# Two attentions on one core: how the projections load x and weights

## The chip, the cores and the metric

The kernel runs on one NeuronCore of a Trainium2 chip. The core has five engines with instruction streams of their own: TensorE (PE: matmuls; its weight loads are listed apart as PEld), VectorE (DVE), ScalarE (ACT), GpSimd (POOL) and SyncE (SP, which here only issues DMAs). Engines wait for one another through semaphores, and each runs its own stream strictly in order. The metric is the device time of one execution in microseconds (us); less is better.

## What is computed

Two attention layers over 2048 rows of width 576, each with 32 heads of 18, on different inputs; the outputs stand side by side. A is a multi-query attention: one key head and one value head serve all 32 query heads. B is cut into 4 segments of 512 rows: within a segment causal attention, and beside it a memory M that earlier segments' keys and values have filled.

```python
q = heads(x @ wq); k = x @ wk; v = x @ wv                        # A
o = softmax(q k^T * Dh**-0.5) v
a = o @ wo

q, k, v = heads(x @ wq), heads(x @ wk), heads(x @ wv)            # B
for s in range(4):
    a_dot = softmax(qs ks^T * Dh**-0.5 + causal) vs
    a_mem = (phi(qs) M) / (phi(qs) z + 1e-6)
    o = g * a_mem + (1 - g) * a_dot                              # g = sigmoid(beta)
    M, z = M + phi(ks)^T vs, z + sum(phi(ks))
b = o @ wo
```

## The kernel before

It has two phases. The *projections* make q, k and v of A and B and write most of them to DRAM; this ends near 320 us. The *attention* phase follows, with an order of instructions written out by hand. The change touches the first only, in which a scheduler orders the instructions of each engine: it may move a DMA or an operation to another place in its engine's stream, ahead of or behind work of neighbouring steps.

**Precision.** Each fp32 operand is split in two parts (fp32r): the cast (high part) and the difference (low part). x gives `xh` and `xl`, weights give `wAh`, `wAl` (A) and `wBh`, `wBl` (B). The contraction over 576 runs in blocks k = 0 to 4 of 128 rows, the last of them 64 rows, loaded twice so that high and low part share it. `proj` (L201, its matmuls at L208) therefore makes an output tile of up to 126 x 512 by 14 matmuls: three for each of k = 0 to 3 (high by high, low x by high weight, high x by low weight) and two for k = 4.

**Loading x.** `next_x(xT, c)` (L186) allocates `xh` and `xl` for 512 rows and returns a function that loads one block k: `load_xk` (L175) takes one of three `xr` buffers of 128 x 512, starts the DMA on SP (L179), casts on DVE (L180) and subtracts on DVE (L182; L184 for k = 4, where there are two DMAs of 64 rows).

**Loading weights.** `load_wk` (L192) takes one of two `wr` buffers, starts the DMA on SP (L195), casts on ACT (L196) and subtracts on POOL, or on DVE for A's first weights (L197).

**A, chunks c = 0 to 3 of 512 rows** (from L221). For c = 0 the five blocks of weights and x are loaded and split in turn. Then five tiles t = 4, 0, 1, 2, 3, each: 14 matmuls into a PSUM tile `pj` (4 buffers); for t = 4 the magnitude (L237), a copy of the values (`vT`, L239) and four transposes (L242); the absolute value for a bound on ACT (`AQ`, L244); `split2` (L106: cast on ACT at L110, subtraction on DVE at L111) into `qp` (2 buffers), and `store_parts` (L114), a DMA on SP at L115. After each tile one block of the next chunk's x is loaded and split, and in chunks 2 and 3 also one block of B's weights (columns 504 to 1152 and 1152 to 1728). At the end of chunk 0 ACT issues the constants (L257 to L262), a row of ones to DRAM (L263, from `onest`) and five tiny loads of beta (L267), and takes beta's exponential (L270).

**Boundary from A to B.** A small matmul with `sel` (L280), DVE operations for `kbdA` (L284), 20 matmuls (L289), and from their result the shift, split in parts (L120 to L123) and stored by four DMAs on ACT (L295).

**B, segments s = 0 to 3** (from L325). Five tiles of keys and queries: 14 matmuls each, the column magnitude `kmB` (L360) and its product with a mask (L364), `split2`, stores, and `phi` (L308 and L309 on ACT, L311 on DVE) whose result `kf` is transposed by PE (L338) and copied (L339). In segment 0 one more block of weights (columns 0 to 504) is loaded after each tile. Then the values (L396 to L401), transposes of the last key head (L409), and four query tiles.

At the very start PE runs nine matmuls on a tile of zeros (`zero`, L160).

Of the kernel before, what the change touches and what calls it, by code (L numbers as in the profile page):

```python
# [7 lines left out]
F32 = mybir.dt.float32  # L8
# [4 lines left out]
ALU = mybir.AluOpType  # L13
# [7 lines left out]
C = 512  # L21
# [47 lines left out]
def attention_pair_kernel(ctx, tc, a_xT, a_w, a_wo, b_xT, b_w, b_wo, b_beta, ident_d, hmask_d, bmask_d, cmask_d, sel_d, zmask_d, selx_d, sely_d, out):  # L69
# [75 lines left out]
    with ExitStack() as ph:  # L145
# [2 lines left out]
        pt = ph.enter_context(tc.tile_pool(name="pt", bufs=2))  # L148
        ps = ph.enter_context(tc.tile_pool(name="ps", bufs=1, space=PSUM))

        onest = pt.tile([32, 128], F32, name="onest", bufs=1)
        nc.gpsimd.memset(onest, 1.0)


        zero = pt.tile([128, C], F32, name="r1", bufs=2)
        nc.vector.memset(zero, 0.0)
        zero = zero.bitcast(BF)
        pz = ps.tile([128, C], F32, name="nd", bufs=2)
# [10 lines left out]
        def halves(k):  # L169

            if k < 4:
                return [(slice(0, 128), slice(128 * k, 128 * k + 128))]
            return [(slice(0, 64), slice(512, 576)), (slice(64, 128), slice(512, 576))]

        def load_xk(xh, xl, xT, c, k):  # L175
            t0 = c * C
            xr = px.tile([128, C], F32, name="xr", bufs=3)
            for rows, src in halves(k):
                nc.sync.dma_start(xr[rows], xT[src, t0 : t0 + C])  # L179
            nc.vector.tensor_copy(xh[:, k], xr)  # L180
            if k < 4:
                nc.vector.tensor_tensor(xl[:, k], xr, xh[:, k].bitcast(F32), op=ALU.subtract)  # L182
            else:
                nc.vector.tensor_tensor(xh[64:128, k], xr[64:128], xh[64:128, k].bitcast(F32), op=ALU.subtract)  # L184

        def next_x(xT, c):  # L186

            xh = px.tile([128, 5, C], F32R, name="xh")
            xl = px.tile([128, 4, C], F32R, name="xl")
            return xh, xl, lambda k: load_xk(xh, xl, xT, c, k)  # L190

        def load_wk(wh, wl, w, c0, n, k, first):  # L192
            wr = pt.tile([128, 648], F32, name="wr", bufs=2)
            for rows, src in halves(k):
                nc.sync.dma_start(wr[rows, :n], w[src, c0 : c0 + n])  # L195
            nc.scalar.copy(wh[:, k, c0 : c0 + n], wr[:, :n])  # L196
            (nc.vector if first else nc.gpsimd).tensor_tensor(  # L197
                wl[:, k, c0 : c0 + n], wr[:, :n], wh[:, k, c0 : c0 + n].bitcast(F32), op=ALU.subtract
            )
# [20 lines left out]
        kAp = p1.tile([128, 1], F32, name="kAp")  # L220
        for c in range(NCH):  # L221
            if c == 0:
                xh, xl, fillx = next_x(a_xT, 0)
                for k in range(5):
                    load_wk(wAh, wAl, a_w, 0, CA, k, True)
                    fillx(k)
                nc.sync.dma_start(ident, ident_d)
            else:
                xh, xl = nx[:2]
            nx = next_x(a_xT, c + 1) if c < NCH - 1 else next_x(b_xT, 0)  # L230
            for t in (4, 0, 1, 2, 3):
                M = 114 if t == 4 else 126
                pj = ps.tile([128, C], F32, name="pj", bufs=4)
                proj(pj[:M], wAh, wAl, xh, xl, 126 * t, M)
                R = RT[t]
                if t == 4:
                    nc.vector.tensor_reduce(km[:M, c : c + 1], pj[:M], axis=AX.X, op=ALU.max, apply_absolute_value=True)  # L237
                    vT = p1.tile([128, C], F32, name="vT", bufs=2)
                    nc.scalar.copy(vT[96:114], pj[96:114])  # L239
                    pv = ps.tile([128, 4, 128], F32, name="tr", bufs=1)  # L240
                    for i in range(4):
                        nc.tensor.transpose(pv[:, i, 0:DH], vT[96:114, 128 * i : 128 * i + 128], ident[96:114, 96:114])  # L242
                    nc.vector.tensor_copy(VAv[:, 4 * c : 4 * c + 4, 1:VW], pv[:, :, 0:DH])
                nc.scalar.activation(AQ[:R, t, c * C : c * C + C], pj[:R], AF.Abs)  # L244
                R2 = 90 if t == 4 else 126
                qp = split2(pt, pj[:R2], R2)
                store_parts(qp, 0, R, qA[c], H0[t], HT[t])
                nx[2](t)

                if c == 2:  # L250
                    load_wk(wBh, wBl, b_w, 504, 648, t, False)
                if c == 3:
                    load_wk(wBh, wBl, b_w, 2 * D, D, t, False)
                if t == 4:
                    nc.sync.dma_start(kA[:, :, c * C : c * C + C], qp[72:90].bitcast(F32))
            if c == 0:
# [3 lines left out]
                nc.scalar.dma_start(zmask[:126], zmask_d)  # L260
                nc.scalar.dma_start(selx[:126], selx_d)
                nc.scalar.dma_start(sely, sely_d)  # L262
                nc.scalar.dma_start(ones_d.rearrange("j (a b) -> (j a) b", b=128), onest)  # L263
                nc.vector.memset(gt, 0.0)
                for t in range(5):
                    lo, nh = H0[t], HT[t]
# [33 lines left out]
        Mbd = p2.tile([128, 5, 7, VW], F32, name="Mbd")  # L300
        Mst = p2.tile([128, 5, 7, DH], F32, name="Mst")
        zst = p2.tile([128, 5, 32], F32, name="zst")
        zc = p2.tile([128, 5], F32, name="zc")

        def phi(src, R, nm, bufs):
# [19 lines left out]
        for s in range(NSEG):  # L325
            xh, xl = nx[:2]
            last = s == NSEG - 1
            if not last:
                nx = next_x(b_xT, s + 1)
            kmB = p2.tile([128, 5], F32, name="kmB", bufs=2)  # L330
            kbB = p2.tile([128, 5, 32], BF, name="kbB", bufs=2)
            pkN = p2.tile([128, 5, 4, 126], F32, name="pkN")
# [24 lines left out]
            for t in range(5):  # L357
# [9 lines left out]
                    store_parts(qp, 72, 54, kB[s], 28, 3)  # L367
                    magnitude(4, pj)
                if s == 0:
                    load_wk(wBh, wBl, b_w, 0, 504, t, False)  # L370
                elif not last:
                    nx[2](t)
                if not last or t == 4:
# [660 lines left out]
```

## Time and profile before

| what | value |
| --- | --- |
| runs | 1475.27, 1481.17 and 1477.9 us, median 1477.9 |
| profiled execution, its own time | 1475.97 us |
| its span in the profile | 1474.3 us |
| projections | 0 to about 320 us |
| attention phase | from there to the end |

The profile is one execution. A window's row gives, for a stretch of time, each engine's busy time with its number of instructions, the granted TensorE clock (1.00 is full), the mean busy share of the 16 DMA engines and the GB/s that they moved. A wait's row names the waiting engine and line, what released it, and the waits' total, number and longest, in us. A timeline row is start, duration, engine (a q behind its name is its queue of DMA issues), line, operation, output and input; in brackets the idle time ahead of it and what ended it. A group's row has the number of instructions, their busy time in us and mean in ns, and the idle time before them with what ended it. In the page's slices each digit is the busy tenth of one fortieth of the span.

### The profile page before, as it was taken

The page shows a single profiled execution, that of the slowest core. Times are in us where ns is not written, and L with a number is a line of the kernel's source. Part 1 is how long each engine was busy: PE and PEld are TensorE (multiplying, and loading weights), DVE is VectorE, ACT ScalarE, POOL GpSimd, SP SyncE. Part 2 cuts the span into 40 slices and gives each one's busy share as a digit, 9 for nine tenths or more (in the row PEclk, how much of TensorE's full clock was granted, in tenths as well). Part 3 has the DMA queues.
Part 4 walks back from the last instruction along what each step waited for, and adds up shares of the span by engine and source line. Part 5 has one row for each costly group of instructions (what it writes and reads, how often), then busy time and mean ns, then how long its engine had stood idle before and what let it go on. Part 6 is the DMA issues. An engine that isn't in the chain of part 4 may idle for free.

```text
span 1474.3 us, 40745 instructions
## 1 busy us (share of the span) xinstructions
PE 1428.2 (97%) x17540; PEld 838.0 (57%) x17540; DVE 1031.0 (70%) x1209; ACT 1193.5 (81%) x1424; POOL 256.0 (17%) x311
## 2 busy tenths in 40 slices
PE   7989999998999999999999999999999999999988
PEld 5768878764544555555555555555555555555554
DVE  6574664555767668887777787777778877887841
ACT  3334334248999999999999999999999999999950
POOL 1031000001134413511110270131115200100010
PEclk9999999999999999999999999999999999999999
DMA  6775643446346345432322343123203121110111
GB/s 197 250 241 179 188 152 122 155 156 192 119 137 200 90 124 160 152 108 86 96 79 75 95 139 105 54 92 98 78 28 120 56 65 49 42 53 17 33 66 62
DMA packets 87985, 166.31 MB, mean 113 GB/s; under 512 B 12479, under 2 KB 21241, under 8 KB 87625
## 3 DMA queue, kind: packets, MB, share of 16 engines
q1 hardware_dynamic: 81510, 157.82, 34.5%
q10 hardware_dynamic: 6291, 5.85, 1.2%
q8 instruction: 138, 2.26, 0.7%
q14 instruction: 46, 0.38, 0.1%
HBM read 96.15 MB, written 67.49 MB: 111 GB/s over the span
## 4 chain that ended last, share of the span: by engine, by line
PE 61%; ACT 9%; DMA 4%; issue 2%; DVE 1%; SPq 1%; POOL 0%; DVEq 0%; POOLq 0%; ACTq 0%
PE O L810 28%; PE E L762 18%; PE F L660 12%; ACT P L780 9%; PE E L771 3%; DMA stB<-qB 2%; PE E L660 1%; DMA oB<-oe 1%; DMA stB<-kB 1%; SPq L586 0%; DVE osb L684 0%; DMA stA<-qA 0%; DVE W L777 0%; PE O L660 0%; DVE oe L819 0%
## 5 line engine op out<-in xcount | busy, mean ns | idle before, releaser
L780 ACT ACTIVATE P<-E 128x1024 f32<-128x1024 f32 (+1 forms) x800 | 784.3, 1068 | 19.7 <-PE E L762 11.2
L777 DVE COPY W<-E 128x1024 f32<-128x1024 f32 (+1 forms) x384 | 461.0, 1200 | 192.4 <-PE E L762 123.4
L810 PE MATMUL O<-P,VA 128*32 128x256 f32 x7936 | 509.2, 380 | 4.9 <-DVE oe L819 4.9
L780 ACT ACTIVATE P<-W 128x1024 f32<-128x1024 f32 (+1 forms) x384 | 430.7, 1122 | 3.3 <-DVE W L777 3.1
L810 PEld LDWEIGHTS O<-P,VA 128*32 128x32 f32 x7936 | 261.9, 110 | 152.8 <-issue 10.8
L762 PE MATMUL E<-stA,kstA 56*128 56x512 f32 x1920 | 328.7, 439 | 1.9 <-ACT P L780 1.0
L762 PEld LDWEIGHTS E<-stA,kstA 56*128 56x128 f32 x1920 | 154.6, 184 | 177.2 <-ACT P L780 113.6
L785 POOL TENSOR_SCALAR_AFFINE_SELECT P<-P 128x256 f32<-128x256 f32 (+1 forms) x192 | 93.7, 493 | 423.0 <-ACT P L780 390.3
L660 PE MATMUL F<-woB,o 126*32 126x192 f32 (+1 forms) x1920 | 127.4, 338 | 0.3 <-DVE osb L684 0.3
L742 DVE SCALAR_TENSOR_TENSOR q<-q,PD 128x1024 f32<-128x1024 f32 x96 | 118.3, 1232 | 0.0
L660 PE MATMUL F<-woA,o 126*32 126x192 f32 (+2 forms) x1480 | 88.7, 337 | 5.8 <-DVE osb L684 5.8
L810 PE MATMUL O<-P,vseg 128*32 128x256 f32 (+2 forms) x1536 | 83.7, 348 | 1.9 <-POOL P L785 1.8
L644 POOL TENSOR_TENSOR o<-oc,rb 126x512 f32<-126x512 f32 (+1 forms) x20 | 26.2, 1323 | 341.6 <-PE F L660 248.3
L110 ACT CAST qp<-pj 126x512 fp32r<-126x512 f32 (+1 forms) x56 | 32.6, 584 | 63.0 <-DVE kmB L360 45.2
L660 PEld LDWEIGHTS F<-woB,o 126*32 126x32 f32 (+1 forms) x1920 | 38.2, 108 | 71.8 <-issue 62.1
L819 DVE COPY oe<-O 128x512 f32<-128x512 f32 x64 | 44.3, 692 | 49.2 <-PE O L810 42.5
L111 DVE TENSOR_TENSOR qp<-pj,qp 126x512 fp32r<-126x512 f32 (+1 forms) x56 | 38.2, 687 | 54.4 <-ACT qp L110 54.2
L208 PE MATMUL pj<-xh,wBh 128*126 128x512 f32 x180 | 73.8, 414 | 2.1 <-DVE xh L180 2.1
L208 PE MATMUL pj<-xh,wBl 128*126 128x512 f32 x180 | 72.9, 405 | 0.0
L771 PE MATMUL E<-stB 56*128 56x256 f32 (+3 forms) x512 | 62.9, 352 | 6.9 <-DMA stB<-kB 2.8
L810 PEld LDWEIGHTS O<-P,vseg 128*32 128x32 f32 x1536 | 48.6, 110 | 28.7 <-POOL P L785 3.9
L660 PEld LDWEIGHTS F<-woA,o 126*32 126x32 f32 (+1 forms) x1480 | 34.8, 108 | 51.9 <-issue 34.6
(135 smaller groups left out, 1439.9 us busy)
## 6 DMA issues: line engine op xcount, KB each, us to landing
stB<-kB SPq DMA_DIRECT2D x96, 144.0 KB
stB<-qB SPq DMA_DIRECT2D x32, 288.0 KB
stA<-qA SPq DMA_DIRECT2D x30, 288.0 KB
oA<-oe SPq DMA_DIRECT2D x32, 256.0 KB
oB<-oe SPq DMA_DIRECT2D x32, 256.0 KB
qA<-qp SPq DMA_DIRECT2D x16, 504.0 KB
kB<-qp SPq DMA_DIRECT2D x16, 504.0 KB
qB<-qp SPq DMA_DIRECT2D x16, 504.0 KB
```

What stands on the lines that cost most here:

```text
L110: nc.scalar.copy(qp[:R, 0, :n], src)
L111: nc.vector.tensor_tensor(qp[:R, 1, :n], src, qp[:R, 0, :n].bitcast(F32), op=ALU.subtract)
L208: nc.tensor.matmul(dst, w[:, c0 : c0 + M], x, start=i == 0, stop=i == len(ops) - 1)
L660: nc.tensor.matmul(dst[32 * j : 32 * j + 32], parts[ab, c][: RT[t], t, r0 : r0 + 32], wo[ab][: RT[t], t, c0 : c0 + n], start=start, stop=stop,
L742: steps.append(lambda a=a: v.scalar_tensor_tensor(q, q, a, p, op0=ALU.add, op1=ALU.mult))
L762: nc.tensor.matmul(e[:, j], kstA[rows, 128 * kt : 128 * kt + 128], st[rows, h, :], start=True, stop=True)
L771: nc.tensor.matmul(e[:, j, c0 : c0 + 512 - 128 * k], st[rows, 4 + h, ks], st[rows, h, 128 * k :], start=True, stop=True)
L777: nc.vector.tensor_copy(src[:, :, :n], e[:, :, :n])
L780: nc.scalar.activation(p[:, :, :n], src[:, :, :n], AF.Exp, scale=SCALE)
L785: nc.gpsimd.affine_select(diag, diag, pattern=[[0, 2], [0, m], [1, 128]], base=0, channel_multiplier=-1, compare_op=ALU.is_ge, fill=0.0)
L810: nc.tensor.matmul(o[32 * j : 32 * j + 32, q0 : q0 + n], v, p[:, j % 2, p0 : p0 + n], start=m == hf == 0, stop=last and hf == 1,)
L819: nc.vector.tensor_copy(osb, o)
```

## The change

- x: a new `raw_x` allocates one `xr` tile for all five blocks of 512 rows (128 x 5 x 512, one buffer) and starts its six DMAs on SP together, at the beginning of the chunk or segment before the one that uses it (for chunk 0: in turn with its weights). `next_x` only casts and subtracts, at the places where load and split stood.
- Weights: `raw_wk` starts the loads on ACT's queue, all five blocks of a group together, into five buffers (`wr` in pool `p1` for A's weights and the first two groups of B's, `qf` in `p2` for the third). They stand at the beginning of chunks 2 and 3 and of segment 0; `split_wk` does the cast and the subtraction at the old places.
- Room: `vT` has one buffer instead of two; the tile of zeros takes the name `sht` with one buffer; `onest` is made and stored at the start of B instead of at the start of the kernel and the end of chunk 0.

The arithmetic is the same.

```diff
         pt = ph.enter_context(tc.tile_pool(name="pt", bufs=2))
         ps = ph.enter_context(tc.tile_pool(name="ps", bufs=1, space=PSUM))
-        onest = pt.tile([32, 128], F32, name="onest", bufs=1)
-        nc.gpsimd.memset(onest, 1.0)
-        zero = pt.tile([128, C], F32, name="r1", bufs=2)
+        zero = pt.tile([128, C], F32, name="sht", bufs=1)
         nc.vector.memset(zero, 0.0)
         zero = zero.bitcast(BF)
         pz = ps.tile([128, C], F32, name="nd", bufs=2)
...
                 return [(slice(0, 128), slice(128 * k, 128 * k + 128))]
             return [(slice(0, 64), slice(512, 576)), (slice(64, 128), slice(512, 576))]
-        def load_xk(xh, xl, xT, c, k):
-            t0 = c * C
-            xr = px.tile([128, C], F32, name="xr", bufs=3)
-            for rows, src in halves(k):
-                nc.sync.dma_start(xr[rows], xT[src, t0 : t0 + C])
-            nc.vector.tensor_copy(xh[:, k], xr)
-            if k < 4:
-                nc.vector.tensor_tensor(xl[:, k], xr, xh[:, k].bitcast(F32), op=ALU.subtract)
-            else:
-                nc.vector.tensor_tensor(xh[64:128, k], xr[64:128], xh[64:128, k].bitcast(F32), op=ALU.subtract)
-        def next_x(xT, c):
+        def raw_x(xT, c, engine, parts=range(5)):
+            xr = px.tile([128, 5, C], F32, name="xr", bufs=1)
+            def load(k):
+                for rows, src in halves(k):
+                    engine.dma_start(xr[rows, k], xT[src, c * C : c * C + C])
+            for k in parts:
+                load(k)
+            return xr, load
+        def next_x(xr):
             xh = px.tile([128, 5, C], F32R, name="xh")
             xl = px.tile([128, 4, C], F32R, name="xl")
-            return xh, xl, lambda k: load_xk(xh, xl, xT, c, k)
-        def load_wk(wh, wl, w, c0, n, k, first):
-            wr = pt.tile([128, 648], F32, name="wr", bufs=2)
+            def fill(k):
+                nc.vector.tensor_copy(xh[:, k], xr[:, k])
+                if k < 4:
+                    nc.vector.tensor_tensor(xl[:, k], xr[:, k], xh[:, k].bitcast(F32), op=ALU.subtract)
+                else:
+                    nc.vector.tensor_tensor(xh[64:128, k], xr[64:128, k], xh[64:128, k].bitcast(F32), op=ALU.subtract)
+            return xh, xl, fill
+        def raw_wk(wr, w, c0, n, k):
             for rows, src in halves(k):
-                nc.sync.dma_start(wr[rows, :n], w[src, c0 : c0 + n])
+                nc.scalar.dma_start(wr[rows, :n], w[src, c0 : c0 + n])
+            return wr
+        def split_wk(wr, wh, wl, c0, n, k, first):
             nc.scalar.copy(wh[:, k, c0 : c0 + n], wr[:, :n])
             (nc.vector if first else nc.gpsimd).tensor_tensor(
                 wl[:, k, c0 : c0 + n], wr[:, :n], wh[:, k, c0 : c0 + n].bitcast(F32), op=ALU.subtract
...
         kAp = p1.tile([128, 1], F32, name="kAp")
         for c in range(NCH):
             if c == 0:
-                xh, xl, fillx = next_x(a_xT, 0)
+                xr, loadx = raw_x(a_xT, 0, nc.sync, ())
+                xh, xl, fillx = next_x(xr)
                 for k in range(5):
-                    load_wk(wAh, wAl, a_w, 0, CA, k, True)
+                    loadx(k)
+                    wr = raw_wk(p1.tile([128, 648], F32, name="wr", bufs=5), a_w, 0, CA, k)
+                    split_wk(wr, wAh, wAl, 0, CA, k, True)
                     fillx(k)
                 nc.sync.dma_start(ident, ident_d)
             else:
                 xh, xl = nx[:2]
-            nx = next_x(a_xT, c + 1) if c < NCH - 1 else next_x(b_xT, 0)
+            nx = next_x((raw_x(a_xT, c + 1, nc.sync) if c < NCH - 1 else raw_x(b_xT, 0, nc.sync))[0])
+            if c > 1:
+                w0, wn = ((504, 648), (2 * D, D))[c - 2]
+                wrs = [raw_wk(p1.tile([128, 648], F32, name="wr", bufs=5), b_w, w0, wn, k) for k in range(5)]
             for t in (4, 0, 1, 2, 3):
                 M = 114 if t == 4 else 126
                 pj = ps.tile([128, C], F32, name="pj", bufs=4)
...
                 R = RT[t]
                 if t == 4:
                     nc.vector.tensor_reduce(km[:M, c : c + 1], pj[:M], axis=AX.X, op=ALU.max, apply_absolute_value=True)
-                    vT = p1.tile([128, C], F32, name="vT", bufs=2)
+                    vT = p1.tile([128, C], F32, name="vT", bufs=1)
                     nc.scalar.copy(vT[96:114], pj[96:114])
                     pv = ps.tile([128, 4, 128], F32, name="tr", bufs=1)
                     for i in range(4):
...
                 nx[2](t)
                 if c == 2:
-                    load_wk(wBh, wBl, b_w, 504, 648, t, False)
+                    split_wk(wrs[t], wBh, wBl, 504, 648, t, False)
                 if c == 3:
-                    load_wk(wBh, wBl, b_w, 2 * D, D, t, False)
+                    split_wk(wrs[t], wBh, wBl, 2 * D, D, t, False)
                 if t == 4:
                     nc.sync.dma_start(kA[:, :, c * C : c * C + C], qp[72:90].bitcast(F32))
             if c == 0:
...
                 nc.scalar.dma_start(zmask[:126], zmask_d)
                 nc.scalar.dma_start(selx[:126], selx_d)
                 nc.scalar.dma_start(sely, sely_d)
-                nc.scalar.dma_start(ones_d.rearrange("j (a b) -> (j a) b", b=128), onest)
                 nc.vector.memset(gt, 0.0)
                 for t in range(5):
                     lo, nh = H0[t], HT[t]
...
         Mbd = p2.tile([128, 5, 7, VW], F32, name="Mbd")
         Mst = p2.tile([128, 5, 7, DH], F32, name="Mst")
         zst = p2.tile([128, 5, 32], F32, name="zst")
+        onest = p2.tile([32, 128], F32, name="onest")
+        nc.gpsimd.memset(onest, 1.0)
+        nc.scalar.dma_start(ones_d.rearrange("j (a b) -> (j a) b", b=128), onest)
         zc = p2.tile([128, 5], F32, name="zc")
         def phi(src, R, nm, bufs):
...
             xh, xl = nx[:2]
             last = s == NSEG - 1
             if not last:
-                nx = next_x(b_xT, s + 1)
+                nx = next_x(raw_x(b_xT, s + 1, nc.sync)[0])
+            if s == 0:
+                wrs = [raw_wk(p2.tile([128, C], F32, name="qf", bufs=5), b_w, 0, 504, k) for k in range(5)]
             kmB = p2.tile([128, 5], F32, name="kmB", bufs=2)
             kbB = p2.tile([128, 5, 32], BF, name="kbB", bufs=2)
             pkN = p2.tile([128, 5, 4, 126], F32, name="pkN")
...
                     store_parts(qp, 72, 54, kB[s], 28, 3)
                     magnitude(4, pj)
                 if s == 0:
-                    load_wk(wBh, wBl, b_w, 0, 504, t, False)
+                    split_wk(wrs[t], wBh, wBl, 0, 504, t, False)
                 elif not last:
                     nx[2](t)
                 if not last or t == 4:
```

## The prediction

> **What bounds the kernel now.** I read the page's first two parts, then the seven stages up to 320 us by windows, then each engine's waits in the first 125 us, then the order of instructions of both kernels.
>
> ```profile
> span 1474.3 us, 40745 instructions
> PE 1428.2 (97%) x17540; PEld 838.0 (57%) x17540; DVE 1031.0 (70%) x1209; ACT 1193.5 (81%) x1424; POOL 256.0 (17%) x311
> PE   7989999998999999999999999999999999999988
> ```
> ```profile
> 0.00:30.35 30.35, 22.97 (x83) 15.10 (x84) 18.71 (x35) 10.03 (x16) 3.92 (x8) 0.94 0.71 201
> 30.35:47.23 16.88, 16.87 (x75) 13.15 (x74) 10.20 (x18) 6.85 (x12) 0.32 (x1) 1.00 0.67 211
> 47.23:64.64 17.41, 17.12 (x76) 12.98 (x75) 8.90 (x16) 6.87 (x12) 0.00 (x0) 1.00 0.75 236
> 64.64:84.48 19.84, 17.25 (x75) 13.06 (x74) 13.99 (x17) 8.11 (x14) 7.87 (x5) 1.00 0.74 234
> 84.48:106.52 22.04, 17.28 (x79) 11.67 (x78) 16.96 (x33) 8.32 (x15) 7.32 (x6) 0.92 0.81 268
> 106.52:123.00 16.48, 15.71 (x95) 14.21 (x96) 12.47 (x20) 8.68 (x22) 4.15 (x4) 0.90 0.72 222
> 123.00:320.00 197.00, 197.00 (x1071) 155.15 (x1069) 104.58 (x234) 69.73 (x143) 1.05 (x3) 1.00 0.48 154
> ```
>
> TensorE (PE) bounds the whole: 97% busy. The first four rows are the A chunks 0 to 3, the fifth is the boundary from A to B up to the first transposes of B's phi keys (L338), the sixth the rest of B's segment 0 up to L409. The columns after the length are PE, weight loads, VectorE (DVE), ScalarE (ACT), GpSimd (POOL), then granted clock, DMA share and GB/s. Length less PE's busy time: 7.4, 0.0, 0.3, 2.6, 4.8, 0.8, 0.0 us; 15.8 us idle before 123 us and none from there to 320. At half clock PE counts as busy, so what the clock cost is apart: 0.06, 0.08 and 0.10 of stages one, five and six, some 1.7 us in each.
>
> In the order of the two kernels all five engines run the same sequence from the L409 transposes on. So what the change brings must be decided before 123 us; after that it is a shift. Its ceiling is 15.8 + 3 x 1.7, about 21 us (1.4%).
>
> ```profile
> PE tr L338 <- DVE kf L311: 3.1, 2, 2.6
> PE pj L208 <- DVE xh L180: 2.9, 4, 1.9
> PE pj L208 <- ACT wAh L196: 2.3, 2, 1.2
> PE pj L208 <- DVE xl L182: 1.5, 1, 1.5
> PE pj L208 <- DVE qp L111: 1.4, 1, 1.4
> ```
>
> These are PE's waits (us in total, times, longest). Late x blocks (L180, L182) cost 4.4, late weights 2.3; the phi chain at the boundary (L311) 3.1, and that is no load at all.
>
> **The change, part by part.**
>
> *Chunk 0.* All five w blocks get buffers of their own and go out on ACT's queue; SP carries x alone.
>
> ```profile
> 1.26 0.42 SPq L179 DMA_DIRECT2D xr<-a_xT  x1
> 6.30 0.49 PE L208 MATMUL pj<-xh,wAh 128*114 128x512 f32 x1 [1.09 <-ACT wAh L196]
> 9.45 1.29 DVE L182 TENSOR_TENSOR xl<-xr,xh 128x512 fp32r<-128x512 f32 x2
> 11.36 0.43 DVE L180 CAST xh<-xr 128x512 fp32r<-128x512 f32 x1 [0.62 <-DMA xr<-a_xT]
> 13.04 1.52 DVE L197 TENSOR_TENSOR wAl<-wr,wAh 128x618 fp32r<-128x618 f32 x2 [0.53 <-ACT wAh L196]
> 13.87 1.22 SPq L195 DMA_DIRECT2D wr<-a_w  x2
> 18.09 0.71 ACT L196 CAST wAh<-wr 128x618 fp32r<-128x618 f32 x1 [0.82 <-DMA wr<-a_w]
> 20.00 0.69 DVE L184 TENSOR_TENSOR xh<-xr,xh 64x512 fp32r<-64x512 f32 x1
> ```
> ```profile
> 64.00:76.00 12.00, 10.49 (x45) 7.71 (x43) 6.92 (x8) 2.73 (x6) 3.38 (x2) 1.00 0.87 288
> 76.00:80.00 4.00, 2.92 (x15) 2.29 (x15) 3.21 (x4) 3.95 (x8) 1.59 (x1) 1.00 0.19 41
> 40.02 0.39 PE L208 MATMUL pj<-xh,wAl 128*126 128x512 f32 x1
> 40.25 0.39 PE L208 MATMUL pj<-xh,wAh 128*126 128x512 f32 x1
> ```
>
> Today the fifth weight block is issued only at 13.87 (two buffers) and cast at 18.09. Changed: x of 5 x 256 KB and three w of 309 KB (from the tiles' shapes) leave at once, 2.2 MB; at the 288 GB/s of a crowded stretch that is 7.7 us, landed near 9.2. The other two w leave behind ACT's first casts, near 9.4; by today's 13.87 to 18.09 they can be cast 4.2 us on, 13.6, before DVE comes to them. DVE's new order puts the fill of x block 3 ahead of the first wAl, so PE, after its first few matmuls at 6.3, stands until 9.2 + 0.43 + 0.76, about 10.4. The fourth wAl is the ninth DVE operation from 9.2 on: casts of 0.43 twice, wAl of 0.76 four times (1.52 for two), xl of 0.65 twice (1.29 for two), 0.69 once: 5.9, so 15.1. After it come 49 of the chunk's 74 matmuls, one per 0.23 us (40.02 to 40.25): 11.3, end 26.4. The new gap of 3.7 us is longer than any of PE's waits above, and I expect a half-clock spell behind it like the three of today: 1.7, end 28.1. Against 30.35: -2.2. Bounds: no spell and landing 1 us earlier -5.0; a spell and landing 2 us later 0.
>
> *Chunk 1.*
>
> ```profile
> ACT gt L270 <- DMA gt<-b_beta: 3.4, 1, 3.4
> ACT wBh L196 <- DMA wr<-b_w: 17.3, 6, 5.5
> ACT qp L110 <- DMA qA<-qp: 11.2, 8, 2.8
> SPq L195 <- POOL wBl L197: 6.4, 6, 2.4
> ```
>
> The beta loads are now issued behind the weights, the last one among chunk 0's evacuations in ACT's order, so they land near the chunk's end; the exponential on ACT (L270, a 3.4 us wait today in the idle start) waits for them in front of evacuations. Four pj buffers give three tiles' lead, 3 x 14 x 0.23 = 9.7 us, so a wait of that size is covered; +0.2 for tiles that meet a thin lead, bounds 0 (the chunk has no idle to give) and +3.4 (the wait bare).
>
> *Chunks 2 and 3.* Today the B weights are issued one tile ahead, after POOL's split freed a buffer (6.4 us of waits on SP), and ACT stands 17.3 us for them. Changed, the five blocks go out far ahead, from ACT. x for the next 512 rows goes out as one group at the chunk's start; its single buffer is free once the last fill of the chunk before is done. The hole from 76 to 80 us (DMA share 0.19) between crowded stretches shows that today's transfers are late by order of issue, not by bytes. Floor for both chunks: twice chunk 1's 16.87 is 33.7 against 37.25, -3.5. I take -2.8: one thin wait per chunk stays. Bounds 0 and -3.5. Moved issues: 18 of b_w at 0.42 are 7.6 us from SP's queue to ACT's, over stages in which ACT is busy 6.9 to 8.3 of 17 to 22 us; covered.
>
> *Boundary.*
>
> ```profile
> 84.48 0.28 PE L280 MATMUL mm<-kmx,sel 114*126 114x1 f32 x2
> 85.54 1.26 PE L289 MATMUL nd<-AQ,kbdA 126*32 126x512 bf16 x20
> 96.01 0.96 PE L208 MATMUL pj<-xh,wBh 128*126 128x512 f32 x3 [1.92 <-DVE xh L180]
> 103.16 0.68 DVE L111 TENSOR_TENSOR qp<-pj,qp 126x512 fp32r<-126x512 f32 x1
> 106.52 0.62 PE L338 MATMUL tr<-ident,kf 126*128 126x126 f32 x4 [2.62 <-DVE kf L311]
> L360 DVE TENSOR_REDUCE kmB<-pj 126x1 f32<-126x512 f32 x5 | 3.4, 687 | 0.5 <-PE pj L208 0.5
> L239 ACT COPY vT<-pj 18x512 f32<-18x512 f32 x4 | 2.3, 578 | 2.9 <-DVE km L237 2.9
> ```
>
> With x present, PE runs from T (84.48 today) through L280 and L289 (1.5) and four key tiles (56 x 0.23 = 12.9): done at T+14.4 without the 1.92 us wait and the spell behind it. But DVE's new order puts the kmB reduction of the fourth tile (0.69) and its small product (0.2) ahead of the first tile's qp subtraction; from that subtraction to the transposes passes 106.52 - 103.16 = 3.4 today. T+18.7, against T+22.04; I add 0.3 for semaphores: -3.0. The stall at L338 itself thus grows, 2.6 to about 4.5 us: DVE's order is late next. On ACT six w issues, the moved ones_d store and four shA stores stand ahead of the first B evacuation; at 0.42 each 4.6 us, done well before T+14. Bounds: +2.0 (two of those stores wait as the 3.2 us below), -6.5 (the 4.8 idle and 1.7 of clock all gone, which DVE's order nearly forbids).
>
> *The rest to 123 us*: one half-clock spell today, one after: 0, bounds +1.5 and -1.7. Memset, vT's single buffer and the renamed zero tile: 0, one operation each in engines with idle time; vT, if bare, 0.6.
>
> **Sum:** -2.2 + 0.2 - 2.8 - 3.0 + 0 = -7.8. The profiled execution took 1475.97 us (its span 1474.3 and 1.7 around it), 1.9 below the median 1477.9 of runs from 1475.27 to 1481.17. 1477.9 - 7.8 = **1470**.
>
> **The rivals.**
>
> *R1: the DMA engines set the pace.* GB/s times length give 14.7 MB for chunks 2, 3 and the boundary; at 288 GB/s that is 51 us, against 53.5 by my sum (33.7 + 0.7 + 19.0 + rounding) and 59.3 today. For it: hardly any slack, and a share of 0.81 already. Against: part of it can go earlier, into chunk 1 with its 0.67. If transfers keep today's mean pace (14.7 MB in 59.3 us, 248 GB/s), these stages gain nothing and chunk 0 alone is left: -2.2 + 0.2, 1476. The Trainium skill, DMA: Bandwidth & Descriptors, "Issuing engines are not separate DMA queues", says that DMAs started by scalar, sync or gpsimd share the same 16 DMA engines, so another queue saves only sequencer time; no run yet shows which holds here, and by it R1 would be the outcome.
>
> *R2: it doesn't load ahead.* One x buffer instead of three blocks: the next group can't leave before the last fill, 1.3 MB take 4.6 us at 288 GB/s, and the first fill comes one tile (3.2 us) into a chunk. DVE then stands some 2 us per chunk; the pj lead of 9.7 hides one such stand, which is against it. Where they come through bare, four groups (chunks 1 to 3 and B's first) give back 4 x 2 = 8 and the time is 1478.
>
> *R3, slower: ACT stands behind its DMA issues.*
>
> ```profile
> 96.64 0.68 ACT L196 CAST wBh<-wr 128x576 fp32r<-128x576 f32 x1 [4.30 <-DMA wr<-b_w]
> 100.50 0.59 ACT L110 CAST qp<-pj 126x512 fp32r<-126x512 f32 x1 [3.18 <-DMA shA<-shp]
> ```
>
> Each issue waits for an earlier transfer to release its completion semaphore and, on ACT, holds the evacuations behind it, hence the pj buffers, hence PE. Waits of 3 to 4 us on transfers occur on ACT today. A stage leaves ACT about 10 us; six issues fit while each waits under 1.6 us. At 3.2 each, three stages lose 3 x (19.2 - 10) = 27.6, less the 9.7 of lead once: +17.9, less chunk 0's 2.2 and the boundary's 3.0: 1477.9 + 12.7, about 1490. Against it: in the new order most of these semaphores belong to transfers issued a whole tile before.
>
> *R4, more:* no spell in chunk 0 and none behind the boundary stall: -7.8 - 3.4 and chunks 2, 3 at the floor -0.7: 1466.
>
> **How the numbers follow.** Within 0.5% (7.4 us: 1470.5 to 1485.3) is about what a measurement can't tell from no change. Forecast 0.52 (own range 1466 to 1474; just over half of it under 1470.5), R4 0.13, R1 0.14, R2 0.08, R3 0.13. Faster: 0.30 + 0.13 = 0.43; same: 0.22 + 0.14 + 0.08 = 0.44; slower 0.13. Range: all lower bounds together are -16.7, 1461; R4's own spread ends near 1463, and above, 1484 leaves R3 out: 1462 to 1484.
>
> **What would show it.** Right: chunk ends near 28, 45, 62, 80 us; a PE gap from about 6.7 to 10; x fills gone from PE's waits after chunk 0; the L338 wait on L311 at 4 to 5 us; L338 near 99 and L409's stage unchanged. R1: DMA share over 0.9 in chunks 2 and 3 with waits on x or weights. R3: ACT's largest waits on DMA in front of L244 or L110, and PE waiting for qp's chain. Wrong altogether: any change in PE's busy share after 123 us.

## The result and the profile after

The changed kernel took 1484.5 us (median of 6 runs, 1482.3 to 1485.5) against 1476.8 us for the kernel before (6 runs, 1474.5 to 1481.2): ratio 1.0043 with a 95% interval of 1.0027 to 1.006, slower by 0.4%. The forecast was 1470, in a range of 1462 to 1484. The profiled execution of the changed kernel has a span of 1482.1 us, 7.8 more than the one before.

Windows of the changed kernel, cut where PE begins chunks 1, 2, 3, the boundary (the matmul with `sel`, now L294), the first phi transposes (now L357) and the transposes of the last key head (L409 before, now L428). Columns as in the windows before. Some lines have new numbers in the changed kernel: a weight's load, cast and subtraction are L201, L205 and L206, x's load and cast L178 and L190, the matmuls of `proj` L217, the copy `vT` and its transposes L254 and L257, `AQ` L259, phi's last step L328.

```profile
0.00:29.18 29.18, 25.21 (x83) 16.95 (x84) 16.77 (x33) 8.65 (x13) 0.29 (x5) 1.00 0.63 180
29.18:49.95 20.77, 17.24 (x76) 12.80 (x74) 12.35 (x20) 9.83 (x18) 6.26 (x4) 1.00 0.88 278
49.95:72.99 23.04, 19.09 (x74) 14.90 (x75) 13.16 (x17) 8.79 (x16) 10.27 (x7) 0.85 0.79 254
72.99:89.76 16.77, 16.77 (x75) 13.15 (x74) 9.71 (x19) 6.83 (x12) 0.00 (x0) 1.00 0.61 197
89.76:110.59 20.83, 14.73 (x80) 10.86 (x78) 14.68 (x33) 5.92 (x12) 2.99 (x4) 0.96 0.88 272
110.59:129.36 18.77, 16.11 (x91) 14.36 (x92) 8.08 (x13) 8.67 (x20) 3.75 (x3) 0.86 0.68 215
129.36:325.00 195.64, 195.41 (x1057) 153.25 (x1054) 102.91 (x230) 69.84 (x144) 1.05 (x3) 1.00 0.44 143
```

Stage by stage against the kernel before:

| stage | before, us | after, us | difference | predicted |
| --- | --- | --- | --- | --- |
| chunk 0 | 30.35 | 29.18 | -1.2 | -2.2 |
| chunk 1 | 16.88 | 20.77 | +3.9 | +0.2 |
| chunks 2, 3 | 17.41, 19.84 | 23.04, 16.77 | +5.6, -3.1 | -2.8 together |
| boundary, to the first phi transposes | 22.04 | 20.83 | -1.2 | -3.0 |
| to the last key head's transposes | 16.23 | 18.77 | +2.5 | 0 |
| the rest of the span | 1351.55 | 1352.74 | +1.2 | 0 |

Chunk 3 runs without a gap; chunks 1 and 2 pay for it, and more. Of chunk 2's 5.6 us, 3.7 are idle time of PE and 2.0 are pace: PE was busy for 19.09 us with 74 matmuls in place of 17.12 with 76, and the granted clock was 0.85 in place of 1.00, behind a gap of 3.9 us. Times of the last key head's transposes and of a small matmul at the end of the projections, the first two rows before, the others after:

```profile
122.75 0.50 PE L409 MATMUL tr<-ident,kn 128*18 128x128 f32 x3 [0.28 <-DVE pkN L339]
317.74 0.27 PE L319 MATMUL nd<-ident,fm 128*1 128x128 f32 x1
```
```profile
129.36 0.49 PE L428 MATMUL tr<-ident,kn 128*18 128x128 f32 x3
325.02 0.27 PE L336 MATMUL nd<-ident,fm 128*1 128x128 f32 x1
```

6.6 us at the first point, 7.3 at the second, 7.8 at the end: most of it is decided before 130 us.

PE's waits in the first 130 us of the changed kernel:

```profile
PE tr L357 <- POOL wBl L206: 6.1, 1, 6.1
PE tr L257 <- ACT vT L254: 3.9, 1, 3.9
PE pj L217 <- DVE qp L111: 3.5, 2, 2.4
PE tr L357 <- DVE kf L328: 2.6, 1, 2.6
PE pj L217 <- DVE wAl L206: 1.9, 1, 1.9
```

The waits for x have left PE's list. They have not left the kernel: DVE, which casts the next chunk's x among other work, stands 16.2 us for it in the first 130 us, and stood 13.7 before. What came in their place are waits for evacuations (qp, vT, phi). Two chains of the timeline show how the first two stalls in A come about:

```profile
26.14 0.68 ACTq L281 DMA_DIRECT2D gt<-b_beta  x1
33.07 0.21 ACT L284 ACTIVATE gt<-gt 128x5 f32<-128x5 f32 x1 [2.76 <-DMA gt<-b_beta]
33.59 0.59 ACT L110 CAST qp<-pj 126x512 fp32r<-126x512 f32 x1 [0.30 <-DVE gt L285]
34.95 0.50 PE L217 MATMUL pj<-xh,wAh 128*126 128x512 f32 x1 [2.38 <-DVE qp L111]
...
56.58 0.59 ACT L110 CAST qp<-pj 126x512 fp32r<-126x512 f32 x1 [4.97 <-DMA qA<-qp]
57.42 0.43 DVE L190 CAST xh<-xr 128x512 fp32r<-128x512 f32 x1 [3.35 <-DMA xr<-a_xT]
59.08 0.58 ACT L254 COPY vT<-pj 18x512 f32<-18x512 f32 x1 [0.71 <-DVE km L252]
59.71 0.61 PE L257 MATMUL tr<-ident,vT 18*128 18x18 f32 x4 [3.94 <-ACT vT L254]
```

A load of half a kilobyte (beta) issued at 26.1 has landed only at 33; ACT stands for it, then the evacuation, then PE. Later ACT stands 5.0 us for a store that has to free `qp`, and DVE 3.4 us for x. Both are transfers. The DMA share in chunk 1 is 0.88 at 278 GB/s where it was 0.67 at 211.

At the boundary, ACT's queue (rows with q) and what stands behind it:

```profile
92.44 0.33 ACTq L201 DMA_DIRECT2D qf<-b_w  x1
93.56 1.58 ACTq L201 DMA_DIRECT2D qf<-b_w  x1
95.54 5.37 ACTq L201 DMA_DIRECT2D qf<-b_w  x3
101.00 4.50 ACTq L309 DMA_DIRECT2D shA<-shp  x4
105.54 0.58 ACTq L201 DMA_DIRECT2D qf<-b_w  x1
106.16 0.59 ACT L110 CAST qp<-pj 126x512 fp32r<-126x512 f32 x1 [10.04 <-DMA shA<-shp]
110.59 1.07 PE L357 MATMUL tr<-ident,kf 126*128 126x126 f32 x4 [6.10 <-POOL wBl L206]
```

From 92.44 to 106.12 ACT does eleven issues, one of them the ones store, and a single cast. The issues by themselves last 8.0 us; the rest is time between them, 3.3 us of it from 96.5 to 99.8. DVE before its first subtraction for B (the first row is the last of five casts of segment 1's x):

```profile
103.79 0.43 DVE L190 CAST xh<-xr 128x512 fp32r<-128x512 f32 x1 [1.44 <-DMA xr<-b_xT]
106.44 0.68 DVE L379 TENSOR_REDUCE kmB<-pj 126x1 f32<-126x512 f32 x1
107.16 0.24 DVE L383 TENSOR_SCALAR kbB<-zmask,kmB 126x32 bf16<-126x32 f32 x1
107.31 1.28 DVE L111 TENSOR_TENSOR qp<-pj,qp 126x512 fp32r<-126x512 f32 x2
```

The releaser named for PE's 6.1 us, POOL, is not the true one: the transposes read `kf`, and that goes back over phi to the qp subtraction at 107.31. This needs ACT's cast, which ended at 106.75, and its turn on DVE, which had stood 1.44 us for segment 1's x and then worked without a gap from 103.79 on. Both were late; DVE came last, by 0.6 us.

### The profile page after: what moved, and what is told of

It is laid out like the page before. It is cut to its first block, busy times and chain, and to the rows that moved or that the text cites. A ratio compares the mean times of both kernels' runs of the same rounds, so it can differ in the third digit from the quotient of the medians.

```text
span 1482.1 us, 40743 instructions
## 1 busy us (share of the span) xinstructions
PE 1433.1 (97%) x17540; PEld 841.5 (57%) x17540; DVE 1024.1 (69%) x1209; ACT 1194.4 (81%) x1424; POOL 260.6 (18%) x311
## 4 chain that ended last, share of the span: by engine, by line
PE 61%; ACT 7%; DMA 4%; issue 2%; DVE 2%; SPq 1%; POOL 0%; DVEq 0%; POOLq 0%; ACTq 0%
PE O L829 28%; PE E L781 17%; PE F L679 12%; ACT P L799 7%; PE E L790 3%; DMA stB<-qB 1%; PE E L679 1%; DVE W L796 1%; DMA woA<-a_wo 1%; DMA oB<-oe 1%; DMA rb<-rB 1%; DMA rB<-sm 0%; DMA stB<-kB 0%; DMA stA<-qA 0%; DVE osb L703 0%
## 5 line engine op out<-in xcount | busy, mean ns | idle before, releaser
L110 ACT CAST qp<-pj 126x512 fp32r<-126x512 f32 (+1 forms) x56 | 32.4, 585 | 81.1 <-DVE kmB L379 45.2
L829 PE MATMUL O<-P,vseg 128*32 128x256 f32 (+2 forms) x1536 | 84.5, 350 | 4.0 <-POOL P L804 3.9
L111 DVE TENSOR_TENSOR qp<-pj,qp 126x512 fp32r<-126x512 f32 (+1 forms) x56 | 38.3, 687 | 61.7 <-ACT qp L110 61.5
L217 PE MATMUL pj<-xh,wBh 128*126 128x512 f32 x180 | 74.0, 411 | 0.0
L217 PE MATMUL pj<-xh,wBl 128*126 128x512 f32 x180 | 71.9, 399 | 0.0
```

The lines of the kernel that those rows point to most:

```text
L110: nc.scalar.copy(qp[:R, 0, :n], src)
L111: nc.vector.tensor_tensor(qp[:R, 1, :n], src, qp[:R, 0, :n].bitcast(F32), op=ALU.subtract)
L217: nc.tensor.matmul(dst, w[:, c0 : c0 + M], x, start=i == 0, stop=i == len(ops) - 1)
L829: nc.tensor.matmul(o[32 * j : 32 * j + 32, q0 : q0 + n], v, p[:, j % 2, p0 : p0 + n], start=m == hf == 0, stop=last and hf == 1,)
```

## The experiments

Theories: A, ACT stands in order behind its DMA issues, and evacuations behind ACT. B, the loads of B's weights now leave a chunk early and their bytes crowd out A's x and stores. C, the single x buffer is to blame. Each edit lets the scheduler reorder all engines, so one stage of one run can differ for other reasons; the conclusions rest on what agrees across runs. All were timed beside the kernel before. The ratios come from 6 to 12 executions; the last two columns come from a single profiled one, which lay up to 4.2 us from the median of its kernel.

| run | ratio to before (95%) | start of B (`sel`), us | from there to the last key head's transposes, us |
| --- | --- | --- | --- |
| before | 1 | 84.5 | 38.3 |
| the change | 1.0043 (1.0027 to 1.0060) | 89.8 | 39.6 |
| e1 weights on SP | 0.9980 (0.9964 to 0.9995) | 79.8 | 41.1 |
| e2 x only | 1.0026 (1.0014 to 1.0038) | 84.4 | 41.5 |
| e3 weights only | 1.0050 (1.0034 to 1.0066) | 92.9 | 37.3 |
| e4 beta late | 1.0025 (1.0012 to 1.0037) | 91.1 | 36.9 |
| e5 weights on POOL | 1.0069 (1.0052 to 1.0086) | 100.9 | 34.9 |
| e6 chunk 0 on SP | 1.0028 (1.0016 to 1.0039) | 89.4 | 39.4 |
| e7 chunks 2, 3 on SP | 1.0000 (0.9987 to 1.0014) | 82.9 | 41.1 |
| e8 segment 0 on SP | 0.9995 (0.9982 to 1.0008) | 86.8 | 34.9 |
| e9 two buffers on ACT | 1.0074 (1.0054 to 1.0094) | 96.6 | 39.0 |
| e10 chunks 2, 3 and segment 0 on SP | 0.9984 (0.9968 to 0.9999) | 85.0 | 38.5 |
| e11 an eighth of the bytes | 0.9982 (0.9968 to 0.9996) | 84.3 | 36.4 |
| e12 held back on ACT | 1.0025 (1.0010 to 1.0041) | 88.5 | 39.0 |
| e13 e1 and the shift stores on SP | 0.9990 (0.9977 to 1.0003) | 79.1 | 48.3 |
| e14 e3 with weights on SP | 0.9987 (0.9972 to 1.0003) | 82.3 | 39.2 |

How far a stage moves without any cause in the edit, e8 shows: up to the start of B every engine runs the same instructions in the same order as in the changed kernel, and yet B starts 3.0 us earlier. A difference of that size in one stage proves nothing. What agrees is this: where ACT issues the whole loads of chunks 2 and 3 into five buffers, B starts at 86.8 us or later (the change, e3, e4, e6, e8, e12); where they come from SP, or bring an eighth of the bytes, at 85.0 or earlier (e1, e7, e10, e11, e13, e14); the means are 89.8 and 82.2. The stage behind it has no such division: 36.4 to 41.1 us with segment 0's loads on ACT in five buffers, 34.9 to 48.3 with them on SP.

**e1, the weights from SP.**

```diff
-                nc.scalar.dma_start(wr[rows, :n], w[src, c0 : c0 + n])
+                nc.sync.dma_start(wr[rows, :n], w[src, c0 : c0 + n])
```

> The changed kernel with the weight loads issued from SP instead of ACT; five buffers and whole x stay. Theory A (ACT stands in order behind its DMA issues): at least 5 of the 7.6 us lost come back, 1476 to 1480, and ACT's 10 us wait in front of B's first evacuation is gone. Theory B (more bytes in flight at once, from whichever queue, make x and stores land late between 30 and 60 us): within 2 us of the changed kernel, 1482 to 1487.

1474.2 us, ratio 0.998: faster than both kernels, and below the range of A. One word of the change carries the whole loss. ACT's 10 us wait at the boundary has become one of 7.0 us, for the shift's parts. But the loads also leave at other times: B's `wr` loads of chunks 2 and 3, the changed kernel first, e1 second (minimum, median and maximum of an issue in ns, first and last start):

```profile
L201 ACTq DMA_DIRECT2D wr<-b_w x12: 329/422/1474, 26.9 to 56.6; - x12
```
```profile
L201 SPq DMA_DIRECT2D wr<-b_w x12: 359/472/2089, 14.5 to 75.9; - x12
```

So e1 speaks against C and does not part A from B.

**e2 and e3, one half of the change alone.** e2 is the kernel before with `raw_x` and the one-buffer zero tile; e3 is the changed kernel with `load_xk` and `next_x` of the kernel before. One place of each edit, e2's first:

```diff
-                nx = next_x(b_xT, s + 1)
+                nx = next_x(raw_x(b_xT, s + 1, nc.sync)[0])
...
-                nx = next_x(raw_x(b_xT, s + 1, nc.sync)[0])
+                nx = next_x(b_xT, s + 1)
```

> The kernel before with only the x part of the change (512 rows at once into one buffer; the zero tile renamed for room). Theory A: nothing is added on ACT, so no loss, 1470 to 1478. Theory B: the x part puts less in flight than both, a part of the loss stays, 1478 to 1483. Third theory C (one x buffer: DVE, in order, stands on x that can only leave after the last fill): most of the loss is here, 1482 to 1487.

> The changed kernel with x loaded block by block into three buffers as before; weights through five buffers on ACT's queue stay. Theory A: the loss stays, 1481 to 1487. Theory B: part of it, 1479 to 1483. Theory C: the loss is gone, 1472 to 1478.

e2: 1481.5 us, a loss of 0.26%, above A's bracket and inside B's. It does not sit where C says: the start of B is that of the kernel before. The stage behind it is 3.2 us longer, which is no more than an execution's own difference, so the seat of this loss stays open. e3: 1484.9 us, as much as the whole change, as A expected. C falls for the chunks; the weights alone are enough.

**e4, beta at the start of B.** The block from the memset of `gt` to `omg` moves:

```diff
+        nc.vector.memset(gt, 0.0)
+        for t in range(5):
+            lo, nh = H0[t], HT[t]
+            nc.scalar.dma_start(
...
         def phi(src, R, nm, bufs):
```

> The changed kernel with the five beta loads, the exponential and the three DVE operations behind it moved from the end of chunk 0 to the start of B. Theory A: ACT no longer stands 7.2 us on an issue of beta and 2.8 us in front of the exponential, DVE not 6.0; 3 to 5 us come back, 1479 to 1482. Theory B: at most 2, 1482.5 to 1487.

1482.2 us, at the edge of what A expected, but its interval overlaps that of the change, and the start of B is no earlier. The stand for beta does not by itself make A late.

**e5, the weights from POOL.**

```diff
-                nc.scalar.dma_start(wr[rows, :n], w[src, c0 : c0 + n])
+                nc.gpsimd.dma_start(wr[rows, :n], w[src, c0 : c0 + n])
```

> The changed kernel with the weight loads issued from POOL, which has little else to do there: they can leave as early as their buffers allow, and no evacuation stands behind them. Theory A (ACT's order): like the weights on SP, 1470 to 1477. Theory B (what hurts is that the loads of chunks 2 and 3 leave a chunk early and crowd x and the stores, which SP's busy queue had prevented): 1480 to 1487.

1489.6 us, ratio 1.0069 (1.0052 to 1.0086): both brackets missed. In its DMA view a load (last column: us from issue to landing) takes

```profile
wr<-b_w POOLq DMA_DIRECT2D x4, 288.0 KB, 8.8
```

and PE and ACT wait for what hangs on it (PE in the first 140 us, then ACT):

```profile
PE tr L257 <- ACT vT L254: 14.7, 3, 7.5
```
```profile
ACT wBh L205 <- DMA wr<-b_w: 9.2, 2, 8.3
```

ACT now stands in front of casts whose weights haven't landed. An engine that does not issue the load can still stand behind it. So taking the issues off ACT is not enough by itself. The run does not decide between A and B, because POOL's late loads are a cause of their own.

**e6, e7, e8, e10, one group or two from SP.** `raw_wk` gets the engine as an argument; e7, for one:

```diff
-                wrs = [raw_wk(p1.tile([128, 648], F32, name="wr", bufs=5), b_w, w0, wn, k) for k in range(5)]
+                wrs = [raw_wk(p1.tile([128, 648], F32, name="wr", bufs=5), b_w, w0, wn, k, nc.sync) for k in range(5)]
```

> The changed kernel with only the weights of chunk 0 issued from SP; those of chunks 2, 3 and segment 0 stay on ACT. The constants and beta can then leave at the start again. Theory A with chunk 0 as the main seat: 1476 to 1480. Theory A with the later groups as the seat: 1481 to 1486.

> The changed kernel with only the weights of chunks 2 and 3 issued from SP; chunk 0 and segment 0 stay on ACT. If the ten loads between chunk 0 and 2 are the seat (ACT standing between evacuations, PE standing 1.2 to 3.9 us for vT and qp there, two half-clock spells), 4 to 7 us come back: 1477 to 1481. If not, 1482 to 1487.

> The changed kernel with only segment 0's weights issued from SP. If the 10 us that ACT stands behind six loads and four shA stores at the boundary is a seat, the 6.1 us wait of PE in front of the first transposes shrinks and 2 to 4 us come back: 1480 to 1482.5. If DVE's order alone sets that wait, within 1 us of the changed kernel.

> The changed kernel with the weights of chunks 2, 3 and segment 0 issued from SP, chunk 0's alone on ACT. If both seats (the early loads of chunks 2 and 3; the stand at the boundary) count by themselves and add up, it takes 1470 to 1474; if the two single moves cured the same us, 1476 to 1480.

Chunk 0's group gives little (1483.1 us). That of chunks 2 and 3 gives 0.43% (1479.3), and its start of B is 6.8 us earlier than the changed kernel's. e7's twelve loads:

```profile
10.85 1.75 SPq L201 DMA_DIRECT2D wr<-b_w  x3
22.14 1.54 SPq L201 DMA_DIRECT2D wr<-b_w  x3
72.21 4.38 SPq L201 DMA_DIRECT2D wr<-b_w  x6
```

None leaves between 24 and 72 us; in the changed kernel ten of the twelve leave from 33 to 57, in chunks 1 and 2. Segment 0's group gives 0.48% (1478.0, more than expected): 4.7 us at the boundary, 34.9 against 39.6, and the 3.0 in front of it that the edit did not cause. By the total times, whose intervals lie apart from the change's, these are the two seats; of the second only that it gains is shown, not how much of it the boundary brings. They do not add up: together 0.59% (1476.6, in the bracket for gains that overlap). e8's times on PE:

```profile
86.80 0.28 PE L294 MATMUL mm<-kmx,sel 114*126 114x1 f32 x2
105.69 0.62 PE L357 MATMUL tr<-ident,kf 126*128 126x126 f32 x4 [4.17 <-POOL wBl L206]
121.73 0.49 PE L428 MATMUL tr<-ident,kn 128*18 128x128 f32 x3
```

**e9, two buffers on ACT's queue.** The lists of five become one load per tile, in two buffers, in all three groups and in chunk 0.

```diff
-                    split_wk(wrs[t], wBh, wBl, 504, 648, t, False)
+                    wr = raw_wk(p1.tile([128, 648], F32, name="wr", bufs=2), b_w, w0, wn, t)
+                    split_wk(wr, wBh, wBl, w0, wn, t, False)
...
```

> The changed kernel with two weight buffers and one load per tile as before, still on ACT's queue; x whole as in the change. Theory B (loads of B's weights that leave a chunk early crowd out x and the stores): they can't leave early, so the start of B (L294) moves from 89.8 to 84 us or earlier and the time to 1476 to 1480. Theory A (standing behind DMA issues on ACT, whatever leaves): no better than the changed kernel, 1482 to 1488, since each issue now also waits for POOL's split on ACT.

1488.7 us, ratio 1.0074 (1.0054 to 1.0094), start of B at 96.6. B's expectation fails; A's holds but for 0.7 us above its range. ACT's waits in the first 135 us:

```profile
ACT wBh L205 <- DMA wr<-b_w: 16.5, 8, 3.0
```

With e1, e2 and the change this gives a square, all with whole x (e2 without the changes of room for `vT` and `onest`): on SP 1.0026 with two buffers and 0.9980 with five; on ACT 1.0074 and 1.0043. Five buffers gain 0.3 to 0.5% on either queue; ACT's queue costs 0.5 to 0.6% with either number.

**e11 and e12, the bytes and their time.** e11 keeps every issue on ACT but loads 72 columns, and the casts and subtractions read them as `wr[:, None, :72].to_broadcast([128, n // 72, 72])`; e12 keeps the bytes and holds the issues back (second part):

```diff
-                wrs = [raw_wk(p1.tile([128, 648], F32, name="wr", bufs=5), b_w, w0, wn, k) for k in range(5)]
+                wrs = [raw_wk(p1.tile([128, 648], F32, name="wr", bufs=5), b_w, w0, 72, k) for k in range(5)]
...
-                wrs = [raw_wk(p1.tile([128, 648], F32, name="wr", bufs=5), b_w, w0, wn, k) for k in range(5)]
+                wrs = [p1.tile([128, 648], F32, name="wr", bufs=5) for k in range(5)]
+                for k in range(5):
+                    nc.gpsimd.tensor_copy(wrs[k][0:128, 0:1], xh[0:128, 0, 0:1].bitcast(F32))
+                    raw_wk(wrs[k], b_w, w0, wn, k)
```

> The changed kernel, in which the loads of B's weights for chunks 2 and 3 bring 72 of 648 and of 576 columns, which the casts and subtractions then read 9 and 8 times over; the issues stay on ACT, as many as before (the output of B differs). Theory B: with an eighth of the bytes the start of B moves from 89.8 to 85 us or earlier, 1476 to 1480. Theory A: the issues on ACT are what counts, the start of B stays at 88 to 91 us, 1481 to 1487.

> The changed kernel in which the loads of B's weights for chunks 2 and 3 stay on ACT, in five buffers and with all their bytes, but may not leave before the first block of that chunk's x is filled (a one-column copy of it on POOL into each buffer). Theory B (the time at which the bytes leave): the first leaves some 10 us later than in the changed kernel, the start of B moves from 89.8 to 87 us or earlier, 1476 to 1482. If the eighth of the bytes helped by its other order of casts alone: 1482 to 1488.

e11: 1475.3 us, 0.7 below B's bracket and outside A's, start of B 5.5 us earlier than the changed kernel's although ACT issues as many loads as before. The twelve issues last 6.3 us together, and 7.2 in the changed kernel, so it is not their own time that went; they are done by 42 us in place of 57. The windows from 30 to 65 us of the changed kernel and of e11:

```profile
30.00:65.00 35.00, 27.52 (x112) 20.66 (x111) 21.67 (x33) 16.67 (x30) 14.37 (x9) 0.90 0.86 275
```
```profile
30.00:65.00 35.00, 31.42 (x132) 24.23 (x131) 25.79 (x35) 17.73 (x31) 15.73 (x10) 0.95 0.70 216
```

PE's idle time there falls from 7.5 to 3.6 us, with as many issues on ACT. But the casts come in another order too. e12's issues, first and last:

```profile
L201 ACTq DMA_DIRECT2D wr<-b_w x12: 334/394/683, 36.7 to 67.0; - x12
```

Though they leave ten us later than in the change, the start of B gains only 1.2 us, and 1483.4 us lies in the bracket for the order of the casts. It clears the bytes no more than it convicts them: the loads still leave while A's x and stores run (36.7 to 67.0). So what is shown is that few bytes in these loads, or SP as their queue, take the loss in A away, and that ten us of delay on ACT do not; how the loss in A divides between bytes and ACT's order stays open.

**e13 and e14, towards a better version.** e13 adds the four shift stores to SP's queue in e1; e14 is e3 with the weights on SP.

```diff
-            nc.scalar.dma_start(shA[c].rearrange("j h t -> h j t"), sp[32 * c : 32 * c + 32].bitcast(F32))
+            nc.sync.dma_start(shA[c].rearrange("j h t -> h j t"), sp[32 * c : 32 * c + 32].bitcast(F32))
```

> The weights on SP with five buffers, whole x, and the four shift stores of A moved from ACT to SP as well, so that ACT doesn't stand 7 us behind them in front of B's first evacuations. If that stand sets the boundary there (41.1 us from L294 to L428 with the weights on SP), it gets 2 to 5 us shorter: 1469 to 1473. If DVE's order sets it: 1473 to 1476, no change.

> x loaded block by block through three buffers as before; weights through five buffers, from SP. If five buffers on SP are what gains (x whole cost 0.26% by itself with two buffers), this is the best of the set, 1469 to 1474. If the gain needs x in one group as well, so that B's weights keep their place behind it on SP, 1476 to 1482.

e13: 1477.2 us, 0.9990 (0.9977 to 1.0003), above both brackets; its start of B is at 79.1, as e1's, and the stage behind it gets longer (48.3 us). e14: 1476.6 us, 0.9987 (0.9972 to 1.0003), in the bracket in which whole x is needed too; but its interval overlaps that of e1, so that is not settled. Of the versions that compute both layers, e1 and e10 have intervals below 1.

## Why the prediction was wrong

*That everything is decided before 123 us and then carried* held within 1.2 us.

*Chunk 0*: -1.2 for -2.2. The gap came (1.9 us in front of the first wAl, not 3.7). Half pace came too, but it stood from the first matmul of `proj`, at 6.1 us, ahead of the gap, and lasted ten us (last section). At 0.43 less 0.23 us for some 19 matmuls that is 3.8 us, an estimate, where the prediction put 1.7.

*Chunks 1 to 3 are the step that failed*: "Changed, the five blocks go out far ahead, from ACT", priced at -2.8 and, for chunk 1, +0.2. Chunk 3 gave what its floor allows, -3.1. The bytes of B's weights went into chunks 1 and 2, and no term charged them there. Length times GB/s: chunk 1 moves 5.8 MB where it moved 3.6, chunk 2 5.9 where it moved 4.1, chunk 3 3.3 where it moved 4.6. Of chunk 1's 2.2 MB more, all are loads of B's weights by its list of issues (3 x 324, 3 x 288 and 2 x 162 KB); of chunk 2's 1.7 MB more only some 0.5 are, the rest is x and stores. At the 288 GB/s of a crowded stretch that the prediction used, 5.8 MB need 20 us, an estimate (from 6 to 10 us the same profile moved 331 GB/s); PE's work there is 17. The prediction's R1 did the sum of bytes, but over chunks 2, 3 and the boundary, and named chunk 1 with its share of 0.67 as the place where some could go for free. That was the error. x and stores pass through the same DMA engines; a late store keeps its `qp` buffer and a late x holds DVE, and both delay the work that frees `pj`. The lead of three tiles (9.7 us) did not cover waits such as 2.8, then 5.0 and 3.4 us. That these loads are the cause is shown (e7 moves them, e11 empties them); how much of it is bytes and how much ACT's order is not. R1's time, 1476, was that of no gain; a loss from the same cause was not among the cases.

*The boundary*: -1.2 for -3.0, and +2.5 behind it for 0. The prediction had the first subtraction for B at T+15.3; it came at T+17.6 (107.31 less 89.76). Two of its terms failed there. One is ACT's: "six w issues, the moved ones_d store and four shA stores stand ahead of the first B evacuation; at 0.42 each 4.6 us, done well before T+14". With the waits between them they took 13.7 us, 1.24 each, and ended at T+16.4 (106.12 less 89.76), no earlier than the same cast stood in the kernel before (100.50 less 84.48, T+16.0). The duration was read from an issue that waited for nothing. The other is DVE's. Segment 0's x was present, and the fourth tile's `kmB` and product stood ahead of the subtraction, as predicted. But ahead of these DVE also had the casts of all five blocks of segment 1's x (two of them in the kernel before), and it stood 4.0 us for their loads; the sum has no term for that. DVE came last, by 0.6 us. The second pair of phi transposes then waited another 2.6 us (L328). In e8 the first cast for B comes at 95.06, T+8.3, eight us sooner, yet the stage is only 1.9 us shorter in front of L357 (and 2.7 behind it): phi still stood behind the shift stores until 101.45, and `kf` behind other work of DVE, which the scheduler had put in another order there. So what the six issues cost by themselves stays open. R3 had ACT's part of this, with 1.6 us per issue as its point of decision; 1.24 was already enough to be late. Its price, 1490, charged three stages with 3.2 us an issue.

*What would show it*: x fills did leave PE's waits; the chunk ends came at 29, 50, 73 and 90 in place of 28, 45, 62 and 80, which tells at once in which chunk the error lies. Of the rivals' signs, R3's came: ACT's largest waits on DMA stood in front of L110 (15.9 us for stores of `qp`) and `AQ`, and PE waited for the chain of `qp`. But the sign does not convict: e1, faster than both kernels, has 21.9 us of that first wait. R2's came in part, DVE's longer stand for x, yet e3, with three x buffers, loses as much.

The Trainium skill, DMA: Bandwidth & Descriptors, "Issuing engines are not separate DMA queues", says that DMAs started by scalar, sync or gpsimd run on the same 16 DMA engines, and that starting them from several engines saves only the sequencer's time. That the DMA engines are shared, chunk 1 bears out: SP's queue took 53.8% of their time and ACT's 34.2%, together its share of 0.88. But the same loads with the same buffers took 0.998 from SP and 1.0043 from ACT: the engine also decides when loads leave and what waits behind the issue, and here that is worth 0.6%.

## What to carry to other kernels

Work that is moved ahead has to be charged to the stage it moves into: add its bytes to that stage's bytes before calling a prefetch free, above all where stores free the buffers. The choice of queue also sets when a load leaves: from SP, behind x and stores, B's weights left in chunk 0 and at the end of A (e7), and not in the chunks that lost time; that this alone makes SP better here is not shown. And price an issue on a compute engine by the stretch that it stands in: eleven of them took 13.7 us here, waits included, where one that waited for nothing lasted 0.42. Last, one profile is one execution: compare the order of instructions before giving a stage's few us to an edit.

## What the runs showed of the hardware

At the start PE can run at half pace while the granted clock reads 1.00. Timeline of the changed kernel, and windows from 5 to 17 us after and before:

```profile
15.07 0.63 PE L217 MATMUL pj<-xh,wAl 128*114 128x512 f32 x1
15.50 0.63 PE L217 MATMUL pj<-xh,wAh 128*126 128x512 f32 x1
```
```profile
5.00:17.00 12.00, 9.54 (x22) 6.29 (x21) 8.98 (x15) 3.55 (x5) 0.00 (x0) 1.00 0.80 239
```
```profile
5.00:17.00 12.00, 9.21 (x38) 6.33 (x37) 7.24 (x12) 3.30 (x5) 0.00 (x0) 1.00 0.70 190
```

One matmul per 0.43 us instead of 0.23 until 16.4 us, 22 matmuls where the kernel before did 38 in about the same busy time. The profiles of e1 to e4 show such matmuls too at the start, up to 13 or 14 us, also at a clock of 1.00; the profile before shows none there. In e7 matmuls at the same spacing come with a clock that shows them:

```profile
10.00:14.00 4.00, 3.12 (x7) 2.37 (x8) 3.97 (x8) 1.42 (x2) 0.00 (x0) 0.50 0.90 282
```

So the clock column tells of the start in some profiles and not in others; the spacing of matmuls tells of it in all of them.
